# A PSUM evacuation moved ahead of an exponential, the first two blocks moved ahead of the third block's transposes, and narrower attention-value matmuls

## The chip, the cores and the metric

One core of one Trainium2 chip. The time is that of the device, in microseconds (us), from run to run of the same program. A kernel that is compared is run several times in turn with the kernel before on the same chip. Each run also lists the mean clock that TensorE was granted (1 is full speed). A run more than 1.5% above the fastest of its kernel counts as slow and stays out of the ratios.

Engines are named as the profile names them: PE is TensorE's matmuls, PEld its weight loads, ACT is ScalarE, DVE is VectorE, POOL is GpSimd, SP is SyncE. L203 is line 203 of a kernel.

## The reference, cut to what matters

Attention with 4 sink keys and a window of 128 keys, followed by a highway layer on the result:

```python
# q, k, v: (4, 8, 768, 64); n_sink = 4, window = 128; w_h, w_t: (512, 512)
scores = scale * np.matmul(q, k.transpose(0, 1, 3, 2))
keep = is_sink | in_window
scores = np.where(keep, scores, -1e9)
a = np.exp(scores - max); a = a / sum(a)
x = np.matmul(a, v)                      # then (B, S, H*D) as (3072, 512)
H = np.maximum(x @ w_h, 0.0)
T = 1.0 / (1.0 + np.exp(-(x @ w_t + b_t)))
return T * H + (1.0 - T) * x
```

## The kernel before

The 3,072 tokens are 24 blocks of 128, six for each of the four sequences. Block `n` sees itself and block `n-1`; from the third block of a sequence on it also sees the four sink keys. The stages of a block are spread over five iterations of one loop (`pe_T` of block `n` at `i = n-2`, `dve_d` at `i = n+2`), and the program fixes the order of each engine's instructions:

```python
for i in range(-2, NB + 2):
    if has_sink(i): act_sink(i)          # ACT L226: exponential of the sink scores of i, i+1
    if on(i + 1):
        pe_S(i + 1, 0)                   # PE  L243: scores of four heads
        act_S(i + 1, 0)                  # ACT L251: first exponential
        pe_S(i + 1, 1)
    ...pe_X(i - 1); act_X(i - 1)         # PE  L310 transposes x; ACT L315 copies xT
    for o in os_: dve_d(o)               # DVE L342: reads hps (block i-2)
    if on(i): dve_mask(i, 1)
    if on(i + 1): act_S(i + 1, 1)        # ACT L251: second exponential
    if on(i + 2): pe_T(i + 2)            # PE  L196/L198: transposes q, k into tp
    ...
    if on(i): pe_A(i)                    # PE  L277: attention-value; L283: its sink part
    if on(i + 2): act_T(i + 2)           # ACT L203: q/k copy, tp -> SBUF
    ...dve_mask(i + 1, 0); dve_rec(i); dve_o(i - 2); dve_x(i)
    for m in ms:                         # m = i-1
        pe_Mt(m)                         # PE  L321/L323 -> tps
        act_u(m)                         # ACT L329: tanh, reads tps
        pe_Mh(m)                         # PE  L336 -> hps
    if has_sink(i + 1): pe_sink(i + 1)   # PE  L221 -> sk, two blocks at once
```
(cut; the comments are not in the kernel)

Two more things matter. The PSUM pool `m` has two buffers of one bank, which `xtp`, `tp`, `tps`, `hps` and, in two blocks of six, `sk` take in turn. And each of the 16 attention-value matmuls of a block streams `_AVN` columns, of which the result needs 65:

```python
_AVN = 112
m_ps = ctx.enter_context(tc.tile_pool(name="ps_m", bufs=2, space=PSUM))
...
nc.tensor.matmul(av[:, g, 2 * hl + hh, 0:_AVN], lhsT=e[:, hh, hl, pc, :],
                 rhs=vt[:, 65 * h:65 * h + _AVN], ...)
```

The softmax here doesn't subtract the row's maximum and nothing guards it: scores larger than these inputs give would overflow.

Of the kernel before, what the change touches and what calls it, by code (L numbers as in the profile page):

```python
# [13 lines left out]

_EXP_BIAS = math.log(1.9)

_AVN = 112


@with_exitstack  # L20
def kernel(
# [37 lines left out]
    AHEAD = 8  # L59
# [65 lines left out]
    def load_sink_v(b):  # L125
        nc.gpsimd.dma_start(out=vs_dn[b % 2], in_=v[b, :, 0:NSINK, :])
# [38 lines left out]
    def more_constants():  # L165
        nc.vector.memset(bt16, 0.0)
        nc.vector.memset(ones_row, 0.0)
        nc.vector.memset(ones_row[0:1, :], 1.0)
        for i in range(2):
            nc.vector.memset(ks_bd[i], 0.0)  # L170
            nc.vector.memset(vs_bd[i], 0.0)
            nc.vector.memset(es_t[i], 0.0)
        nc.vector.tensor_copy(out=mask0, in_=mask[:, 1, :])
        nc.vector.memset(mask0[0:NSINK, :], 1.0)
        nc.vector.tensor_copy(out=mask1, in_=mask)
        nc.vector.memset(mask1[0:NSINK, 0, :], 1.0)
        nc.vector.tensor_scalar_mul(bt16[0:1, :], bt32, 0.5)
# [6 lines left out]
    def warm_up(n):  # L184
        w = m_ps.tile([P, DM], FP32, tag="m", name="wps")
        for _ in range(n):
            nc.tensor.matmul(w, lhsT=warm[:, 0:P], rhs=warm, start=True, stop=True)

    qkT, tp_of, s_of, e_of, av_of, rec_of = {}, {}, {}, {}, {}, {}
    xtp_of, xh_of, xT_of, t_of, u_of, h_of, dd_of, ee_of, sk_of = {}, {}, {}, {}, {}, {}, {}, {}, {}  # L190

    def pe_T(n):
        qsd, ksd = qk_sd.pop(n)
        tp = m_ps.tile([P, 2 * NHP, P], FP16, tag="m", name="tp")
        for j in range(NHP):
            nc.tensor.transpose(tp[:, j, :], qsd[:, 2 * j:2 * j + 2, :], ident)  # L196
        for j in range(NHP):
            nc.tensor.transpose(tp[:, NHP + j, :], ksd[:, 2 * j:2 * j + 2, :], ident)  # L198
        tp_of[n] = tp

    def act_T(n):
        qk = qkT_pool.tile([P, 2 * NHP, P], FP16, tag="qk", name="qk")
        nc.scalar.copy(out=qk, in_=tp_of.pop(n))  # L203
        qkT[n] = (qk[:, 0:NHP, :], qk[:, NHP:2 * NHP, :])
# [20 lines left out]
    def act_sink(n):  # L225
        nc.scalar.activation(out=es_t[(n // 2) % 2][0:NS4], in_=sk_of.pop(n)[0:NS4], func=AF.Exp,  # L226
                             bias=ebias[0:NS4], scale=SCALE)

    def srcs_of(n):
        return ([] if n % NSC == 0 else [qkT[n - 1][1]]) + [qkT[n][1]]  # L230

    def pe_S(n, g):
        qT, _ = qkT[n]
        srcs = srcs_of(n)
        np_ = len(srcs)
        sps = s_ps.tile([P, 2, 512], FP32, tag="s", name="sps")
        for hl in range(2):
            hp = 2 * g + hl
            for pc, kk in enumerate(srcs):
                for hh in range(2):  # L240
                    rows = slice(64 * hh, 64 * hh + 64)
                    o = (hl * np_ + pc) * P
                    nc.tensor.matmul(sps[:, hh, o:o + P], lhsT=kk[rows, hp, :],  # L243
                                     rhs=qT[rows, hp, :], start=True, stop=True)
        s_of[n, g] = sps

    def act_S(n, g):
        np_ = 1 if n % NSC == 0 else 2
        sps = s_of.pop((n, g))
        e = e_pool.tile([P, 2, 2, np_, P], FP16, tag="e", name="e")  # L250
        nc.scalar.activation(out=e.rearrange("p a b c d -> p a (b c d)"),  # L251
                             in_=sps[:, :, 0:2 * np_ * P], func=AF.Exp,
                             bias=ebias, scale=SCALE)
        e_of[n, g] = e

    def dve_mask(n, g):
        c = n % NSC
        np_ = 1 if c == 0 else 2
        m = {0: mask0, 1: mask1.rearrange("p a b -> p (a b)")}.get(
            c, mask.rearrange("p a b -> p (a b)"))  # L260
        ev = e_of[n, g].rearrange("p a b c d -> p (a b) (c d)")
        nc.vector.tensor_tensor(  # L262
            out=ev, in0=ev, in1=m.unsqueeze(1).to_broadcast([P, 4, np_ * P]),
            op=ALU.mult)
# [24 lines left out]
    def dve_rec(n):  # L289
        rec = r_pool.tile([P, H], FP32, tag="rec", name="rec")  # L290
        nc.vector.reciprocal(out=rec.unsqueeze(2), in_=av_of[n][:, :, 64:65])
        rec_of[n] = rec
# [13 lines left out]
    def pe_X(n):  # L306
        xh = xh_of[n]
        xtp = m_ps.tile([P, NOC, P], FP16, tag="m", name="xtp")
        for j in range(NOC):
            nc.tensor.transpose(xtp[:, j, :], xh[:, j * P:(j + 1) * P], ident)  # L310
        xtp_of[n] = xtp

    def act_X(n):
        xT = x_pool.tile([P, NOC, P], FP16, tag="xT", name="xT")
        nc.scalar.copy(out=xT, in_=xtp_of.pop(n))  # L315
        xT_of[n] = xT
# [15 lines left out]
    def pe_Mh(n):  # L332
        xT = xT_of.pop(n)
        hps = m_ps.tile([P, DM], FP32, tag="m", name="hps")
        for kc in range(NOC):
            nc.tensor.matmul(hps, lhsT=xT[:, kc, :], rhs=wh_sb[:, kc, :],  # L336
                             start=(kc == 0), stop=(kc == NOC - 1))
        h_of[n] = hps

    def dve_d(n):  # L340
        dd = td_pool.tile([P, DM], FP16, tag="dd", name="dd")
        nc.vector.scalar_tensor_tensor(out=dd, in0=h_of.pop(n), scalar=0.0, in1=xh_of[n],  # L342
                                       op0=ALU.max, op1=ALU.subtract)
        dd_of[n] = dd

    def dve_e(n):
        ee = td_pool.tile([P, DM], FP16, tag="ee", name="ee")
        nc.vector.scalar_tensor_tensor(out=ee, in0=u_of.pop(n), scalar=1.0, in1=dd_of.pop(n),  # L348
                                       op0=ALU.add, op1=ALU.mult)
        ee_of[n] = ee  # L350

    def dve_o(n):
        otok = o_pool.tile([P, DM], FP32, tag="otok", name="otok")
        nc.vector.scalar_tensor_tensor(out=otok, in0=xh_of.pop(n), scalar=2.0, in1=ee_of.pop(n),  # L354
                                       op0=ALU.mult, op1=ALU.add)
        nc.sync.dma_start(out=out[n * P:(n + 1) * P, :], in_=otok)

    def on(n):
        return 0 <= n < NB
# [4 lines left out]
    def highway(i):  # L364
        return [m for m in range(NB) if m + lag(m) == i]

    def has_sink(n):
        return on(n) and n % NSC >= 2 and n % 2 == 0

    with tc.manual_schedule(engines={ENG.PE, ENG.DVE, ENG.Activation, ENG.SP, ENG.Pool}):  # L370
        for i in range(-2, NB + 2):
            ms, os_ = highway(i), highway(i - 1)
            if i == -2:
                warm_up(8)
                more_constants()
            if has_sink(i):
                act_sink(i)
            if on(i + 1):
                pe_S(i + 1, 0)
                act_S(i + 1, 0)  # L380
                pe_S(i + 1, 1)
            if on(i - 1) and i - 1 not in XBAR:
                pe_X(i - 1)
                act_X(i - 1)
            for o in os_:
                dve_d(o)
            if on(i):
                dve_mask(i, 1)
            if on(i + 1):
                act_S(i + 1, 1)  # L390
            if on(i + 2):
                pe_T(i + 2)
            for o in os_:
                dve_e(o)
            if on(i):
                pe_A(i)
            if on(i + 2):
                act_T(i + 2)
            if on(i + 1):
                dve_mask(i + 1, 0)  # L400
            if on(i):
                dve_rec(i)
            for o in os_:
                dve_o(o)
            if on(i):
                dve_x(i)
                if i in XBAR:
                    sp_X(i)
            for m in ms:
                pe_Mt(m)  # L410
                act_u(m)
                pe_Mh(m)
            if has_sink(i + 1):
                pe_sink(i + 1)
            if i == 0:
                sink_ones()
                sink_v(0, nc.vector)
            if on(i + 2) and (i + 2) % NSC == 0:
                b = (i + 2) // NSC
                pool_sink(b)  # L420
                if b:
                    sink_v(b, nc.gpsimd)
                if b + 1 < B:
                    load_sink_v(b + 1)
            for n in (range(3, AHEAD + 1) if i == -2 else [i + 2 + AHEAD]):
                if n < NB:
                    if n > 3:
                        load_qk(n)
                    load_v(n)
# [35 lines left out]
```

## Time and profile before

146.31 us, median of three runs (146.3 to 146.74).

| what | before | how read |
|---|---|---|
| busiest engine | PE, 80% of the span | the page, part 1 |
| ACT | 68% | the page, part 1 |
| PE at half clock | about 11 to 26 us (the prediction reads 28) | the page, row PEclk (a digit is 3.6 us); the H matmuls at 26.65 us are at the full rate again |
| six blocks, steady | 30.0 us | from one sink exponential to the same of the next sequence |

The profile's page of the kernel before, parts 1 and 2: busy time by engine, then tenths of PE's time and of its clock in 40 equal slices.

```profile
PE 115.4 (80%) x1312; PEld 74.8 (52%) x1312; DVE 96.9 (67%) x214; ACT 98.0 (68%) x129; POOL 73.6 (51%) x98
...
PE   6632069989889988988899789889897988998840
...
PEclk9975555899999999999999999999999999999996
```

No engine is full, so something makes them wait for each other. The list of waits of the kernel before says who; its columns are the total us, the times, and the longest:

```profile
DVE dd L342 <- PE hps L336: 26.2, 24, 1.5
...
ACT e L251 <- PE sps L243: 12.7, 16, 0.9
...
PE hps L336 <- ACT qk L203: 9.4, 17, 0.7
...
ACT es L226 <- PE sk L221: 8.1, 8, 1.1
```

And the chain of waits of the kernel before shows the ring, that is, a loop of waits that closes on itself from block to block; start us, us, what:

```profile
83.15 1.11 ACT e L251
84.26 0.47 ACT xT L315
84.74 1.02 ACT e L251
85.75 0.91 ACT qk L203
...
86.71 1.02 PE hps L336 x4
87.73 0.46 PE sk L221 x8
...
88.24 0.35 issue
```

ACT does first exponential, xT copy, second exponential, q/k copy. Only then may PE do the H matmuls, because `hps` takes the buffer of `tp`. The next scores stand behind the H matmuls, and the next first exponential waits for these scores. That is 4.96 us per block, 5.4 where a sink matmul and its exponential come in between. At the start, PE stands still; its timeline of the kernel before, where the last bracket is the idle time and what ended it:

```profile
18.77 0.61 PE L196 MATMUL tp<-ident,qsd 128*128 128x128 f16 x4 [6.70 <-DMA qsd<-in_q_dram]
```

PE works in program order, so the attention of blocks 0 and 1, whose data is long there, stands behind the transposes of block 2, whose q lands at 18.7 us.

### The profile page before, as it was taken

How to read it: one execution, taken by the hardware profiler on the slowest of the kernel's cores; microseconds unless marked ns; L12 is line 12 of the kernel's file. 1: busy time of each engine (PE TensorE's matmuls, PEld its weight loads, DVE VectorE, ACT ScalarE, POOL GpSimd, SP SyncE). 2: the span in 40 equal slices, each digit the busy share in tenths (PEclk: the TensorE clock that was granted, in tenths of full speed). 3: DMA queues.
4: the chain of work that ended last, by engine and by line, in shares of the span. 5: the costliest groups of instructions: out<-in, count | busy, mean ns of one | idle time of the engine just before them, and what ended most of it. 6: DMA issues, size and time to landing. Idle time of an engine off the chain costs nothing.

```text
span 145.0 us, 3266 instructions
## 1 busy us (share of the span) xinstructions
PE 115.4 (80%) x1312; PEld 74.8 (52%) x1312; DVE 96.9 (67%) x214; ACT 98.0 (68%) x129; POOL 73.6 (51%) x98
## 2 busy tenths in 40 slices
PE   6632069989889988988899789889897988998840
PEld 2122058557646654765666358458464664664410
DVE  7441016578659856966868687678677866968770
ACT  3176029497787877977976797798769778976310
POOL 6999599999969999735099770000300000000000
PEclk9975555899999999999999999999999999999996
DMA  1999999999999999999929999210221021021111
GB/s 10 113 112 168 165 155 158 153 156 197 163 190 195 191 183 150 195 194 152 74 74 147 150 197 161 73 73 3 75 77 72 1 77 72 0 77 72 72 72 72
DMA packets 79728, 17.00 MB, mean 117 GB/s; under 512 B 75617, under 2 KB 76641, under 8 KB 79714
## 3 DMA queue, kind: packets, MB, share of 16 engines
q0 software_dynamic: 76256, 10.51, 107.8%
q1 hardware_dynamic: 3458, 6.30, 12.1%
q8 instruction: 10, 0.16, 0.4%
q14 instruction: 4, 0.03, 0.1%
HBM read 21.01 MB, written 6.29 MB: 188 GB/s over the span
## 4 chain that ended last, share of the span: by engine, by line
ACT 41%; PE 35%; POOL 7%; DMA 5%; issue 5%; DVE 4%; POOLq 0%; DVEq 0%
ACT e L251 25%; PE hps L336 16%; ACT qk L203 11%; DMA ksd<-in_k_dram 5%; PE tps L323 4%; ACT xT L315 4%; PE av L277 4%; PE sps L243 4%; DVE dd L342 3%; PE sk L221 3%; POOL qsd L85 2%; PE tps L321 1%; POOL ksd L86 1%; POOL v L93 1%; PE tp L198 1%
## 5 line engine op out<-in xcount | busy, mean ns | idle before, releaser
L251 ACT ACTIVATE e<-sps,ebias 128x1024 f16<-128x1024 f32 (+1 forms) x48 | 49.8, 1041 | 12.7 <-PE sps L243 12.7
L342 DVE SCALAR_TENSOR_TENSOR dd<-hps,xh 128x512 f16<-128x512 f32 x24 | 16.6, 692 | 26.2 <-PE hps L336 26.2
L262 DVE TENSOR_TENSOR e<-e,mask 128x1024 f16<-128x1024 f16 (+1 forms) x48 | 30.7, 640 | 4.4 <-ACT e L251 4.0
L203 ACT COPY qk<-tp 128x1024 f16<-128x1024 f16 x24 | 24.3, 1015 | 11.7 <-PE tp L198 11.7
L336 PE MATMUL hps<-wh_sb,xT 128*128 128x512 f16 x96 | 24.6, 378 | 9.4 <-ACT qk L203 9.4
L85 POOL DMA_DIRECT2D qsd<-in_q_dram x24 | 22.4, 932 | 7.6 <-PE tp L198 5.0
L323 PE MATMUL tps<-wt_sb,xT 128*128 128x512 f16 x96 | 25.0, 383 | 0.0
L277 PE MATMUL av<-v,e 128*128 128x112 f16 x352 | 24.4, 218 | 0.7 <-DVE e L262 0.7
L86 POOL DMA_DIRECT2D ksd<-in_k_dram x24 | 22.2, 925 | 1.1 <-PE av L283 1.0
L93 POOL DMA_DIRECT2D v<-in_v_dram x24 | 22.5, 937 | 0.0
L277 PEld LDWEIGHTS <-e 128*128 128x128 f16 x352 | 21.3, 101 | 1.1 <-DVE e L262 0.9
L336 PEld LDWEIGHTS <-xT 128*128 128x128 f16 x96 | 9.3, 97 | 23.5 <-issue 14.1
L329 ACT ACTIVATE u<-tps 128x512 f16<-128x512 f32 x24 | 14.7, 613 | 6.9 <-PE tps L323 6.8
L243 PE MATMUL sps<-qk 64*128 64x128 f16 x352 | 14.8, 225 | 2.6 <-ACT qk L203 2.6
L348 DVE SCALAR_TENSOR_TENSOR ee<-u,dd 128x512 f16<-128x512 f16 x24 | 16.5, 686 | 0.2
L296 DVE TENSOR_TENSOR xh<-av,rec 128x512 f16<-128x512 f32 x24 | 16.4, 685 | 0.1
L196 PE MATMUL tp<-ident,qsd 128*128 128x128 f16 x96 | 9.9, 230 | 7.2 <-DMA qsd<-in_q_dram 6.9
L354 DVE SCALAR_TENSOR_TENSOR otok<-xh,ee 128x512 f32<-128x512 f16 x24 | 15.6, 648 | 0.1
L243 PEld LDWEIGHTS <-qk 64*128 64x128 f16 x352 | 10.7, 98 | 9.4 <-issue 7.3
L323 PEld LDWEIGHTS <-xT 128*128 128x128 f16 x96 | 9.5, 99 | 11.0 <-issue 1.8
L315 ACT COPY xT<-xtp 128x512 f16<-128x512 f16 x24 | 13.7, 572 | 1.0 <-PE xtp L310 1.0
L212 POOL COPY ks<-qk 64x16 f16<-64x16 f16 x8 | 1.6, 201 | 21.1 <-ACT qk L203 20.9
(49 smaller groups left out, 103.3 us busy)
## 6 DMA issues: line engine op xcount, KB each, us to landing
out_dram<-otok SPq DMA_DIRECT2D x24, 256.0 KB, 2.2
qsd<-in_q_dram POOLq DMA_DIRECT2D x24, 128.0 KB, 5.7
ksd<-in_k_dram POOLq DMA_DIRECT2D x24, 128.0 KB, 5.7
v<-in_v_dram POOLq DMA_DIRECT2D x24, 128.0 KB, 6.1
wt_sb<-in_moe_w_t_dram POOLq DMA_DIRECT2D x1, 512.0 KB, 6.7
wh_sb<-in_moe_w_h_dram POOLq DMA_DIRECT2D x1, 512.0 KB, 8.8
vd<-in_v_dram POOLq DMA_DIRECT2D x4, 4.0 KB, 4.2
bt<-in_moe_b_t_dram SPq DMA_DIRECT2D x1, 2.0 KB
```

Source lines behind the costliest of these rows:

```text
L85: nc.gpsimd.dma_start(out=qsd, in_=q[b, :, rows, :].transpose([1, 0, 2]))
L86: nc.gpsimd.dma_start(out=ksd, in_=k[b, :, rows, :].transpose([1, 0, 2]))
L93: nc.gpsimd.dma_start(out=vt[:, :, 0:D], in_=v[b, :, rows, :].transpose([1, 0, 2]))
L203: nc.scalar.copy(out=qk, in_=tp_of.pop(n))
L243: nc.tensor.matmul(sps[:, hh, o:o + P], lhsT=kk[rows, hp, :], rhs=qT[rows, hp, :], start=True, stop=True)
L251: nc.scalar.activation(out=e.rearrange("p a b c d -> p a (b c d)"), in_=sps[:, :, 0:2 * np_ * P], func=AF.Exp, bias=ebias, scale=SCALE)
L262: nc.vector.tensor_tensor(out=ev, in0=ev, in1=m.unsqueeze(1).to_broadcast([P, 4, np_ * P]), op=ALU.mult)
L277: nc.tensor.matmul(av[:, g, 2 * hl + hh, 0:_AVN], lhsT=e[:, hh, hl, pc, :], rhs=vt[:, 65 * h:65 * h + _AVN], start=first, stop=False, skip ...
L315: nc.scalar.copy(out=xT, in_=xtp_of.pop(n))
L323: nc.tensor.matmul(tps, lhsT=xT[:, kc, :], rhs=wt_sb[:, kc, :], start=False, stop=(kc == NOC - 1))
L336: nc.tensor.matmul(hps, lhsT=xT[:, kc, :], rhs=wh_sb[:, kc, :], start=(kc == 0), stop=(kc == NOC - 1))
L342: nc.vector.scalar_tensor_tensor(out=dd, in0=h_of.pop(n), scalar=0.0, in1=xh_of[n], op0=ALU.max, op1=ALU.subtract)
```

## The change

Three parts. (1) The q/k copy goes ahead of the second exponential on ACT, so that `tp`'s buffer comes free sooner. (2) Up to block 2 the loop is rearranged, so that blocks 0 and 1 are done while block 2's loads are under way. (3) `_AVN` goes from 112 to 80, to take PE time away.

```diff
-_AVN = 112
+_AVN = 80
...
-            if on(i + 1):
+            if i >= 2 and on(i + 1):
                 pe_S(i + 1, 0)
                 act_S(i + 1, 0)
                 pe_S(i + 1, 1)
...
-            if on(i + 1):
+            if i >= 2 and on(i + 2):
+                pe_T(i + 2)
+                act_T(i + 2)
+            if i >= 2 and on(i + 1):
                 act_S(i + 1, 1)
-            if on(i + 2):
-                pe_T(i + 2)
...
                 pe_A(i)
-            if on(i + 2):
-                act_T(i + 2)
...
+            if i == 1:
+                dve_d(0)
+                pe_T(2)
+                act_T(2)
+            if -1 <= i < 2:
+                for g in range(2):
+                    pe_S(i + 1, g)
+                    act_S(i + 1, g)
+                dve_mask(i + 1, 0)
+            if i < 2:
+                n = {-2: 0, -1: 1, 1: 3}.get(i)
+                if n is not None:
+                    pe_T(n)
+                    act_T(n)
```
(cut; the rest follows from it: the guards on what is done early, and the loads of blocks 10 and 11, which keep their order)

More of the change, by code (lines that the diff above doesn't have):

```diff
@@ L385 @@
             for o in os_:
-                dve_d(o)
+                if o not in dd_of:
+                    dve_d(o)
             if on(i):
                 dve_mask(i, 1)
-            if on(i + 1):
+            if i >= 2 and on(i + 2):
+                pe_T(i + 2)
+                act_T(i + 2)
+            if i >= 2 and on(i + 1):
                 act_S(i + 1, 1)
-            if on(i + 2):
-                pe_T(i + 2)
             for o in os_:
@@ L396 @@
                 pe_A(i)
-            if on(i + 2):
-                act_T(i + 2)
-            if on(i + 1):
+            if i >= 2 and on(i + 1):
                 dve_mask(i + 1, 0)
@@ L424 @@
                     load_sink_v(b + 1)
-            for n in (range(3, AHEAD + 1) if i == -2 else [i + 2 + AHEAD]):
+            for n in {-2: range(3, AHEAD + 1), 0: [], 1: [10, 11]}.get(i, [i + 2 + AHEAD]):
                 if n < NB:
```

## The prediction

> **What bounds it now.** No engine is full: busy shares on the page are PE 80%, ACT 68%, DVE 67%, POOL 51%. The chain that ended last is ACT 41%, PE 35%. In the steady part it is a ring through both, read from the chain of waits at 83 to 88 us: first exponential 1.11, xT copy 0.47, second exponential 1.02, q/k copy 0.91, then the H matmuls (L336) 1.02, then the next scores 0.35: 4.96 us per block. The matmuls wait for the q/k copy ("PE hps <- ACT qk" 9.4 us, 17 times, in the list of waits): the PSUM pool "m" has two buffers, and hps takes the one that tp leaves. With a sink matmul it is 5.4, so a pair of blocks with a sink takes 10.4 (first exponentials at 78.19, 88.59, 98.95); six blocks take 30.0 (68.92 to 98.95). Loads don't bind after the start: POOL needs 2.7 us a block. At the start PE has nothing from 12.1 to 18.8 us, waiting for block 2's q, and runs at half clock from about 11 to 28 us.
>
> **The change, costed.**
> 1. q/k copy ahead of the second exponential. Mh may start 1.02 us earlier, so the ring above is cut. Next limits, walked by hand with the trace's durations: (a) ACT back to back: 1.00 + 0.47 + 0.91 + 1.02 + 0.52 = 3.9 us; (b) PE/DVE: Mh 1.05, dd 0.74, transposes 0.44, attention-value, tps 1.08: tp now waits for dd, because dd frees its buffer; (c) xT copy to tps to hps to scores: 1.0 + 0.6 + 1.08 + 0.86 + 0.35 = 3.9. A block without sink: 3.9 to 4.1. A price: the sink matmul needs the PSUM buffer that tanh reads, and tanh is now behind the second exponential, so sink and its exponential no longer hide: about 5.05 with sink. Pair with sink 10.4 -> 9.0; six blocks 30.0 -> 26.0. Over the 20 blocks of the steady part (28.5 to 129 us): -13.5 us, nearly all critical.
> 2. 80 columns: 16 matmuls now start 49 ns apart (0.79 us per block). The Trainium skill, "TensorE: Matmul & The Clock Gate", section "Back-to-back issue gap", gives N/2.4 + 2.5 ns warm: 49 for 112 columns, which this trace confirms; 36 for 80 (estimate; scores go at 28, so weight loads needn't stop it). -0.21 us a block of PE, in ring (b) only: alone about nothing before; after step 1 up to 0.2 us in about half of the blocks (counted above).
> 3. Blocks 0, 1 early. Attention and highway of block 0 and attention of block 1 move into the 6.7 us hole. First exponential of block 3 comes at about 26.5 to 27 instead of 28.54. Against it: Mt and Mh of block 0 wait for weights (wh lands about 18) ahead of block 2's transposes (+0.4), and PE is still cold. Net -1.5.
> Tail unchanged (-0.2).
>
> 146.3 - 13.5 - 1.5 = 131.3; something for hand-overs: **131.5 us, range 128.5 to 135.5**. Faster 0.97, same 0.025, slower 0.005.
>
> **What would show it.** Wait "PE hps <- ACT qk" nearly gone; "ACT e <- PE sps" (12.7 us) mostly gone without sink; new waits of tp (L196) on dd and of sk on tanh; pairs about 9.0 apart; L277 at about 36 ns start to start; ACT busy share up to about 75%; first transposes of block 2 at about 19.8; H matmuls of block 0 before them.
>
> **What would make it wrong.** L277 limited by its weight loads (stays 50 ns: +1 to 2 us). dd late, so ring (b) binds everywhere (+3). PE staying cold past 30 us because the start is more broken up, or block 4's loads (issued about 19, landing 6 to 8 later) not there at 26.5 (+1 to 2). Exponentials and copies slowed by denser PSUM traffic.

## The result and the profile after

133.65 us, median of four runs (132.22 to 135.34), against 146.31 before (four runs). The run at 135.34 counts as slow and is not in the ratio. The ratio is 0.910, with a 95% interval of 0.9015 to 0.9185. Ratios here are the mean time of one kernel's fast runs over that of the other's of the same rounds, so not quite the ratio of the medians. The prediction of 131.5 us with a range of 128.5 to 135.5 holds it, 2 us above the centre.

The four runs differ more than those before, and with the clock: 132.22 us at a mean clock of 0.994, then 133.19, 134.11 and 135.34 at 0.945, 0.943 and 0.924. The profile was taken of the first, and that of the kernel before of a run of 146.7 us, so the spans below differ by more (14.5 us) than the medians (12.7). The same parts of the page, for the changed kernel:

```profile
PE 111.0 (85%) x1312; PEld 70.0 (54%) x1312; DVE 96.6 (74%) x214; ACT 98.3 (75%) x129; POOL 73.4 (56%) x98
...
PE   6757596399999899999998989999989899997820
...
PEclk9999999999999999999999999999999999999997
```

Busy times hardly moved except PE's (4.4 us less); the span shrank around them. The list of waits of the changed kernel:

```profile
DVE dd L342 <- PE hps L336: 14.9, 24, 2.9
...
ACT es L226 <- PE sk L221: 5.3, 8, 0.7
ACT e L251 <- PE sps L243: 3.5, 6, 0.7
...
PE sk L221 <- ACT u L329: 2.1, 7, 0.3
```

The H matmuls' wait for the q/k copy is gone from the list, and a new one is there, the sink matmul's for tanh (7 times). The chain of waits of the changed kernel over two blocks, the first without a sink matmul at its end, the second with one:

```profile
80.56 0.25 PE tps L321
80.82 0.86 PE tps L323 x4
81.68 0.86 PE hps L336 x4
82.54 0.35 PE sps L243 x8
...
82.92 1.07 ACT e L251
...
84.39 1.03 ACT qk L203
85.42 1.02 ACT e L251
86.44 0.50 ACT u L329
...
86.98 0.61 PE sk L221 x8
```

In the chain the first block is now held by PE, though nearly in a tie (the xT copy, which the tps matmuls also need, ends at 80.39 us, 0.05 before they start), and the second by ACT: tanh stands behind the second exponential, and the sink matmul waits for the buffer that tanh reads. First exponentials start at 78.84, 82.92 and 87.99 us: 4.08 us for the block without, 5.07 for the block with a sink matmul.

To see where the time went, the span is cut at the sink exponentials, of which there are eight. The first cut is the second sink exponential (block 4), the last one is the eighth, 18 blocks later; the timeline of ACT gives them.

| stretch (us) | before | changed | difference |
|---|---|---|---|
| start to second sink exponential | 38.52 | 34.48 | -4.04 |
| 18 blocks, second to eighth | 90.08 | 79.71 | -10.37 |
| eighth to the end | 16.4 | 16.3 | -0.1 |
| span | 145.0 | 130.5 | -14.5 |

The start of the changed kernel's PE timeline shows the hole filled; block 0's highway matmuls stand ahead of block 2's transposes, at half speed:

```profile
15.73 0.63 PE L321 MATMUL tps<-bt,ones_row 128*128 128x512 f16 x1
16.15 1.91 PE L323 MATMUL tps<-wt_sb,xT 128*128 128x512 f16 x4
17.85 1.91 PE L336 MATMUL hps<-wh_sb,xT 128*128 128x512 f16 x4
19.56 0.50 PE L196 MATMUL tp<-ident,qsd 128*128 128x128 f16 x4
```

### The profile page after: what moved, and what is told of

It is laid out like the page before. It is cut to its first block, busy times and chain, and to the rows that moved or that the text cites. A ratio compares the mean times of both kernels' runs of the same rounds, so it can differ in the third digit from the quotient of the medians.

```text
span 130.5 us, 3265 instructions
## 1 busy us (share of the span) xinstructions
PE 111.0 (85%) x1312; PEld 70.0 (54%) x1312; DVE 96.6 (74%) x214; ACT 98.3 (75%) x129; POOL 73.4 (56%) x98
## 4 chain that ended last, share of the span: by engine, by line
PE 44%; ACT 23%; DMA 9%; POOL 9%; issue 6%; DVE 6%; POOLq 0%; DVEq 0%
ACT e L251 13%; PE tps L323 11%; PE hps L336 11%; ACT qk L203 6%; DMA qsd<-in_q_dram 6%; PE sps L243 5%; PE av L277 4%; POOL qsd L85 3%; DMA ksd<-in_k_dram 3%; PE tps L321 3%; DVE dd L342 3%; POOL ksd L86 3%; PE sk L221 3%; POOL v L93 2%; ACT xT L315 2%
## 5 line engine op out<-in xcount | busy, mean ns | idle before, releaser
L323 PE MATMUL tps<-wt_sb,xT 128*128 128x512 f16 x96 | 25.5, 389 | 0.1
L336 PE MATMUL hps<-wh_sb,xT 128*128 128x512 f16 x96 | 25.5, 390 | 0.0
L277 PE MATMUL av<-v,e 128*128 128x80 f16 x352 | 19.6, 204 | 2.3 <-DVE e L262 2.3
L329 ACT ACTIVATE u<-tps 128x512 f16<-128x512 f32 x24 | 14.5, 605 | 7.9 <-PE tps L323 7.8
L277 PEld LDWEIGHTS <-e 128*128 128x128 f16 x352 | 17.0, 100 | 3.2 <-DVE e L262 3.0
L348 DVE SCALAR_TENSOR_TENSOR ee<-u,dd 128x512 f16<-128x512 f16 x24 | 16.4, 685 | 0.2
L296 DVE TENSOR_TENSOR xh<-av,rec 128x512 f16<-128x512 f32 x24 | 16.4, 684 | 0.1
L321 PE MATMUL tps<-bt,ones_row 128*128 128x512 f16 x24 | 9.3, 389 | 1.7 <-ACT xT L315 1.0
L198 PE MATMUL tp<-ident,ksd 128*128 128x128 f16 x96 | 9.7, 226 | 1.0 <-DMA ksd<-in_k_dram 1.0
```

What stands on the lines that cost most here:

```text
L296: nc.vector.tensor_tensor(out=xh.rearrange("p (h d) -> p h d", d=D), in0=av_of.pop(n)[:, :, 0:D], in1=rec_of.pop(n).unsqueeze(2).to_broadc ...
L323: nc.tensor.matmul(tps, lhsT=xT[:, kc, :], rhs=wt_sb[:, kc, :], start=False, stop=(kc == NOC - 1))
L336: nc.tensor.matmul(hps, lhsT=xT[:, kc, :], rhs=wh_sb[:, kc, :], start=(kc == 0), stop=(kc == NOC - 1))
```

## The experiments

Theory: the steady gain is the freed `tp` buffer; narrower columns pay only once PE is on the ring; the start gains what the hole allows, less what PE loses to half clock. Rivals: the gain is PE time; or the run-to-run spread is the loads. All results below were correct against the reference. The table has all twelve runs; "first" is the stretch to the second sink exponential, "18 blocks" the steady one, both from the profiled run alone.

| run | median us | ratio to before, 95% | first | 18 blocks |
|---|---|---|---|---|
| copy_only | 137.56 | 0.9447 (0.9389 to 0.9504) | 38.16 | 81.37 |
| cols_only | 145.98 | 1.0052 (0.9953 to 1.0151) | 37.59 | 89.40 |
| start_only | 144.88 | 0.9951 (0.9901 to 1.0002) | 36.48 | 90.04 |
| all_112 | 136.18 | 0.9348 (0.9297 to 0.9399) | 36.54 | 81.56 |
| copy_80 | 135.3 | 0.9252 (0.919 to 0.9315) | 37.48 | 79.72 |
| all_65 | 133.65 | 0.9135 (0.9078 to 0.9191) | 37.73 | 79.43 |
| after_again | 133.13 | 0.9077 (0.903 to 0.9124) | 36.25 | 79.72 |
| warm | 132.45 | 0.9027 (0.8987 to 0.9067) | 34.56 | 79.72 |
| start_warm | 143.97 | 0.9858 (0.9819 to 0.9898) | 36.00 | 90.03 |
| sink_av | 132.16 | 0.8947 (0.888 to 0.9015) | 37.22 | 77.39 |
| sink_av_late | 132.64 | 0.9043 (0.8987 to 0.91) | 36.30 | 78.43 |
| sink_warm | 130.51 | 0.8896 (0.8849 to 0.8943) | 34.51 | 78.14 |

The runs are from three chips, so across rows the ratios and the 18 blocks are to be compared, less so the medians.

### One part at a time

copy_only, the first part alone on the kernel before:

```diff
+            if on(i + 2):
+                pe_T(i + 2)
+                act_T(i + 2)
             if on(i + 1):
                 act_S(i + 1, 1)
-            if on(i + 2):
-                pe_T(i + 2)
...
-            if on(i + 2):
-                act_T(i + 2)
```

> The kernel before with only the q/k copy put ahead of the second exponential, in every block. Theory (the buffer of tp released 1.0 us sooner lets the H matmuls go): about 138.5 us, the wait of the H matmuls for the q/k copy (9.4 us) nearly gone, and a new wait of the sink matmul for tanh. It stays above the full change by the start (about 2) and by the 112 columns (about 2.8). Rival (the gain needs the shorter attention-value matmuls, that is, PE was the limit): over 142 us.

Measured 137.56. The 18 blocks fell from 90.08 to 81.37, 84% of the steady gain (8.71 of 10.37). The wait of the H matmuls for the q/k copy is not in its list of waits any more, and the sink matmul's for tanh is. PE had the same work as before, so the rival falls.

cols_only, `_AVN = 80` alone:

> The kernel before with 80 columns alone. Theory: the attention-value matmuls are not on the ring of before, so 0 to 0.6 us less (start and tail only), though they start 36 ns apart instead of 49. Rival (PE time bounds): 24 x 0.21 = 5 us less.

Measured 145.98, ratio 1.0052 with an interval on both sides of 1. In the profile the 18 blocks are 0.68 us shorter. Nothing like 5 us is there: 24 blocks times 0.21 us of PE work went into PE's waits.

start_only, the rearranged start alone:

> The full change without the new place of the q/k copy from block 2 on and with 112 columns: only blocks 0 and 1 early. Theory: 1.5 to 2.8 us less than before (143.5 to 144.8), all of it ahead of block 3's first exponential. Rival (the weights of the highway layer hold up block 2's transposes and eat the gain): within 0.7 us of before.

Measured 144.88, 0.7 us under before (means 144.85 and 145.59), short of the 1.5 to 2.8 expected; its interval reaches 1.0002, so a gain is not clear of the noise. The steady blocks are as before (90.04). Its clock row shows what happened after the early blocks:

```profile
PEclk9975589699999999999999999999999999999998
```

The clock came back near 19 us and fell again near 26 (slice 8 of 40 reads 6). Between the first and second sink exponential lie 11.32 us (25.16 to 36.48), where 10.36 is usual in this kernel.

all_112, everything but the columns, and all_65, everything with 65 columns:

> The full change with 112 columns kept. Theory: about 136.5 us: blocks without a following sink matmul are bound by PE, 0.21 us each, 4 in 6; blocks with one are bound by ScalarE and the tanh buffer and pay nothing. Rival (columns do nothing): as the full change, 133.7.

> The full change with 65 columns, the least that the result needs. Theory (these matmuls are bound by their columns): they start 30 ns apart, 0.1 us less a block in the blocks bound by PE, about 1 us less than the full change. Rival (80 is already at the floor of the weight loads): start to start stays at 36 ns and the time as the full change.

all_112 measured 136.18: the columns are worth 1.85 us in the 18 blocks (81.56 - 79.71) once the copy has moved (1.65 from copy_only to copy_80), and 0.68 without. The 2.5 us that the expectation's 0.21 us in four blocks of six comes to was not reached. So the parts don't just add up. copy_80 says the same without the early start:

> The kernel before with the q/k copy moved and 80 columns, without the early blocks 0 and 1. Theory: the columns pay about 2 to 2.5 us once the copy has moved (they paid nothing resolved alone): about 135.2 us; what then remains to the full change, about 2, is the start. Rival (the start gives only the 0.7 that it gave alone): 134.

It measured 135.3, and its 18 blocks take 79.72 us, as in the full change; what is left to the full change is the start alone.

With 65 columns the matmuls do start 30 ns apart, as one sees in PE's timeline of all_65 (eight of them and one L283 in 0.36 us, of which L283 is 0.11):

```profile
86.83 0.41 PE L277 MATMUL av<-v,e 128*128 128x65 f16 x8
87.08 0.28 PE L283 MATMUL av<-vs,es 128*128 128x260 f16 x1
87.19 0.41 PE L277 MATMUL av<-v,e 128*128 128x65 f16 x8
```

But the time is 133.65, no less than the full change (three of its four runs have a mean clock of 0.937 or less, so the stages say more), and the 18 blocks gained 0.3 us. The spacing was expected rightly and the gain wrongly: 80 columns already take these matmuls mostly off the ring. The traces show what holds the blocks after that: with 65 columns the tps matmuls start 0.04 to 0.05 us after the end of the xT copy in five blocks of six (83.50 after 83.46), with 80 already 0.04 to 0.07 after it (80.44 after 80.39), while with 112, in copy_only, they start later, behind the attention-value matmuls (85.23 after 85.01).

### The clock at the start

after_again is the changed kernel itself, once more on another chip; warm adds matmuls of zeros, into PSUM that is overwritten afterwards, where PE waits before block 3:

```diff
+    def fill(dst, n):
+        for _ in range(n):
+            nc.tensor.matmul(dst, lhsT=warm[:, 0:P], rhs=warm[:, 0:dst.shape[-1]],
+                             start=True, stop=True)
...
+        if g == 0 and n in (0, 1, 2):
+            fill(sps[:, 0, :], 5)          # in pe_S
...
+        if n == 1:
+            fill(av[:, 0, :, :].rearrange("p h e -> p (h e)"), 4)   # in pe_A
...
+            if n == 2 and t == 1:
+                fill(sk[:, 1, :], 24)      # in pe_sink
```

> The changed kernel once more, unedited, as the yardstick of this chip. Expected: 132 to 135 us, and the shorter runs are those with the higher mean granted clock (0.99 against 0.94), because in the others PE drops back to half clock for some microseconds around block 3.

> The changed kernel with 43 matmuls of zeros put into the waits of PE ahead of block 3 (results overwritten), to keep PE's clock up. Theory (the spread of the changed kernel is the half clock at the start): clock 0.98 or more in all runs, 132 to 132.8 us, spread under 1 us, about 1 us under the unedited kernel. Rival (the spread comes from elsewhere, such as the loads): median and spread as the unedited kernel, or longer by the added work.

after_again: the three runs at 0.994 or 0.995 took 132.51 to 132.91 us, the three at 0.923 to 0.946 took 133.34 to 135.59 (the last counts as slow). Its profile fell on one of the latter, of 133.97. Clock rows of after_again and of warm:

```profile
PEclk9985569859999999999999999999999999999998
```

```profile
PEclk9999999999999999999999999999999999999996
```

In after_again the first to the second sink exponential takes 10.68 us (25.57 to 36.25), in the run that kept its clock 9.16: the second fall costs 1.5 us there. With warm all six runs had 0.985 or more, the median was 132.45 (131.63 to 132.8), and that stretch took 9.16. So the theory stands for the profiled runs; over all runs it is less clear. The spread of 3.1 us became 1.2, a little over the 1 us expected, but without the slow run it was only 1.5, and the mean of the fast runs fell by 0.7 us (133.09 to 132.36) with overlapping intervals.

Two limits. The mean clock does not sort the runs of other kernels: in cols_only the two at 0.994 and 0.995 took 147.0 and 146.68 us, the two at 0.932 and 0.934 only 145.28 and 144.98, so it is a hint and not a proof for runs without a profile. And something else moves the start too: the first sink exponential, about where the second fall sets in, comes between 25.16 and 26.31 us in the profiles with the new start (without sink_av_late, whose sink is moved); whether that is the loads was not tried.

The first fall cost nothing that showed: the changed kernel ran at half rate until 19.6 us, warm did not, and their first sink exponentials come at 25.32 and 25.40. The Trainium skill, "TensorE: Matmul & The Clock Gate", section "Part 1: The HAM clock gate", says that the clock starts at half and goes to full after some 3.4 us of sustained work, in a window that runs freely, so that it differs from run to run. These runs agree: in after_again and warm the first eight matmuls, of 512 columns, take 3.59 us (from 1.26), the half rate, and by 6.5 us the full one is there (four transposes in 0.40 us); the same program kept its clock in some executions and lost it in others, and 512-column matmuls start 0.43 us apart in the half state (four in 1.70 us, from 16.15 to 17.85 above) and 0.21 in the full one. But those 0.43 us fell in a run whose clock row reads 9 everywhere, so the row misses some; the spacing of the matmuls is the surer sign.

start_warm asks whether this also explains start_only:

> start_only with the 43 matmuls of zeros in the waits at the start. start_only gained only 0.7 us, less than the 1.5 to 2.8 expected; its profile shows half clock at 26 to 29 us and 11.3 us between the first two sink exponentials where 10.4 is usual. Theory (that dip ate the rest): clock 0.98 or more, 10.4 us between them, about 143.9 us or 1 us under start_only (ratio to before about 0.983 to 0.988). Rival (the early blocks are worth no more): as start_only, ratio 0.995.

Measured 143.97, ratio 0.9858, clock 0.988 or more in all six runs, and 10.35 us (25.65 to 36.00) between the first two sink exponentials. All as the theory expected, and its interval (0.9819 to 0.9898) lies under that of start_only (0.9901 to 1.0002), though on another chip. The early blocks alone are worth 0.5% by the ratio, not clear of the noise, and 1.4% with the clock kept.

### The price of the copy's new place

With 80 columns, the attention-value tile has free columns. sink_av writes the sink scores there, so that they take no buffer of pool `m`:

```diff
-        sk = m_ps.tile([P, 2, P], FP32, tag="m", name="sk")
+        sk = av_last[0]                   # the av tile of the block just done
...
-                nc.tensor.matmul(sk[:, t, :], lhsT=ks[:, hp * P:(hp + 1) * P],
-                                 rhs=qT[:, hp, :], ...)
+                nc.tensor.matmul(sk[:, t, :, 80:112], lhsT=ks[:, hp * P:(hp + 1) * P],
+                                 rhs=qT[:, hp, :].rearrange("p (a b) -> p a b", b=32), ...)
```
(cut; the exponential reads the same columns, and the comment is not in the kernel)

The first matmul of the sink scores clears accumulate flags in a bank that holds finished results; the Trainium skill, "PSUM — Partial Sum Buffer", section "The four PSUM rules", says that the flags of the bank are cleared, not the data, and the correct result agrees.

> The changed kernel with the sink scores written to the columns 80 to 112 of the attention-value PSUM tile, which the shorter matmuls leave free, so that they take no buffer of pool m and need not wait for tanh. Theory (the price of the copy's new place is that wait): pairs of blocks with a sink 8.8 us instead of 9.16, 2.4 to 2.8 us less in all; no wait of the sink matmul for tanh. Rival (ScalarE's own order holds the sink exponential back anyway): 0.5 us less or nothing.

> As sink_av, and the sink matmul and its exponential put behind the next block's first scores and exponential. Theory: the first exponential no longer waits for the sink, but the attention-value matmuls now wait for the sink exponential (they reuse its PSUM tile): pairs 8.75 us, about 3 us less than the changed kernel, no more than 0.6 better than sink_av. Rival (that wait is hidden): pairs of 8.4 us, 6 us less.

The changed kernel's ACT timeline around a sink exponential:

```profile
85.30 1.14 ACT L251 ACTIVATE e<-sps,ebias 128x1024 f16<-128x1024 f32 x1
86.31 0.62 ACT L329 ACTIVATE u<-tps 128x512 f16<-128x512 f32 x1
87.62 0.47 ACT L226 ACTIVATE es<-sk,ebias 32x256 f16<-32x256 f32 x1 [0.70 <-PE sk L221]
```

and sink_av's (its lines are shifted: L254, L333, L228):

```profile
86.97 1.14 ACT L254 ACTIVATE e<-sps,ebias 128x1024 f16<-128x1024 f32 x1
87.98 0.62 ACT L333 ACTIVATE u<-tps 128x512 f16<-128x512 f32 x1
88.81 0.47 ACT L228 ACTIVATE es<-av,ebias 32x256 f16<-32x256 f32 x1 [0.22 <-PE av L222]
```

The sink exponential starts 0.83 us after tanh instead of 1.31. Pairs of blocks with a sink take 8.79 us (80.02 to 88.81) instead of 9.16, as expected, and the 18 blocks 77.39 instead of 79.72; no wait of the sink matmul for tanh is in its list of waits any more. That confirms the buffer that tanh reads as a price, of about 0.4 us per sink matmul (2.33 us for six); the rest of the 1 us between a block with and one without is not explained by it. The same section of the clock page as cited above ("Architectural detail") calls ACT's queue strict first-in first-out, and the trace agrees: in both kernels tanh starts only 1.01 us after the exponential ahead of it, though in the changed kernel the last tps matmul was followed by the H matmuls at 85.66, 0.65 us before tanh. The whole time gained less than the 2.4 to 2.8 expected (means of the fast runs 131.69 against 133.09 of after_again). Between the two profiled runs the start took 0.97 us of it back (first stretch 37.22 against 36.25, with the clock falling again in both); whether that holds for the other runs is not shown.

sink_av_late puts the sink behind the next first exponential:

```diff
-            if has_sink(i):
-                act_sink(i)
...
                 pe_S(i + 1, 1)
+            if has_sink(i):
+                pe_sink(i)
+                act_sink(i)
...
-            if has_sink(i + 1):
-                pe_sink(i + 1)
```

It is no better: pairs of 8.97 us (8.75 expected), 18 blocks 78.43. The new wait that was expected is in its list, the attention-value matmuls for the sink exponential, but it is short; the matmuls' weight loads waited longer without a cause that the profile names:

```profile
PEld L280 <- issue: 2.1, 7, 0.7
...
PE av L280 <- ACT es L228: 0.6, 1, 0.6
```

Why it is 0.2 us a pair over what was expected is left open.

sink_warm joins sink_av and the matmuls of zeros:

> Both repairs in one: sink scores in the spare columns of the attention-value tile (with the zeros between the two halves of the first one) and the 43 matmuls of zeros at the start. Theory: the two are in different stages and add up: 132.45 (zeros alone) less 8 pairs x 0.36 = about 129.6 us, clock 0.98 or more. Rival (something else takes over in the steady part): 131 or more.

Measured 130.51 us (129.71 to 131.07), ratio 0.8896: the lowest median here (its interval overlaps that of sink_av), and its interval lies wholly under that of the changed kernel. It is 0.9 above what was expected. In the profiled run 0.74 us of that was one event, seen in DVE's and PE's timeline:

```profile
48.15 1.53 DVE L366 SCALAR_TENSOR_TENSOR ee<-u,dd 128x512 f16<-128x512 f16 x1
...
51.61 0.61 PE L227 MATMUL av<-qk,ks 128*128 128x128 f16 x8 [0.59 <-DVE xh L314]
```

One DVE operation took 1.53 us instead of 0.69, and here the sink matmul has to wait for DVE to be done reading the attention-value tile. A second such operation, at 66.44 us, cost its stretch nothing (17.00 us). Both run while POOL does its tensor operation of L129 (47.69 to 49.13 and 66.04 to 67.41 us). That this is the cause was not tried, and whether it happens in each run is open.

## Why the prediction was right, and where its sum was off

- "hps takes the one that tp leaves" and "the ring above is cut": right. copy_only alone gave 84% of the steady gain.
- "About 5.05 with sink": measured 5.07. The price by tanh's buffer was right in kind, and sink_av took about 0.4 us of it away.
- "A block without sink: 3.9 to 4.1": mis-sized, measured 4.08 to 4.25 for blocks with full-size exponentials, and hence six blocks took 26.57 us (25.32 to 51.89), not 26.0, and the steady part of 20 blocks gave 11.6 us (100.44 - 88.87), not 13.5. The term that failed is in ring (c), "0.86 + 0.35" for the H matmuls and the scores up to the next exponential. From the start of the H matmuls to that exponential the changed kernel takes 1.40 us (81.52 to 82.92), not 1.21. The kernel before has the same 1.40 (81.75 to 83.15), so the prediction could have read it there; its chain shows 1.02 + 0.35, which was shortened by hand. Of the 0.19 missing, 0.10 lies ahead of the first scores: they start 0.96 us after the H matmuls (81.52 to 82.48), and four of these take 4 x 0.216 = 0.86. The other 0.09 lies between the first scores and the exponential, 0.44 us (82.48 to 82.92) and not 0.35. The one block of six at 4.25 goes through ring (b), as the prediction allowed for some blocks: in the chain, `dd` at 91.74 us (0.70) releases the transposes at 92.49.
- "80 columns", 49 ns to 36: right. Eight of them and one L283 take 0.40 us (83.77 to 84.17), of which L283 is 0.11. "Alone about nothing": right.
- "Net -1.5" at the start: too small where the clock holds (28.16 to 25.32 for the first sink exponential, 2.84 us in this pair of profiles; over the four with the old start and the nine with the new one, again without sink_av_late, the means are 28.14 and 25.65) and about right where it falls again, which the prediction listed as what would make it wrong; warm and start_warm show it.
- "Tail unchanged (-0.2)": -0.1.

Together: 1.9 us too much in the steady part, 1.3 too little at the start, and about 1.5 for the second clock fall, which by their mean clocks three runs of four had (only one of each kernel's runs has a profile). That makes up the 2 us between 131.5 and 133.65; the 1.5 is measured in after_again and carried over. That the centre came so near is in part luck, since the first two errors offset each other.

The mis-sized term, in PE's timeline of the changed kernel:

```profile
81.52 1.03 PE L336 MATMUL hps<-wh_sb,xT 128*128 128x512 f16 x4
...
82.48 0.62 PE L243 MATMUL sps<-qk 64*128 64x128 f16 x16
...
84.80 1.03 PE L323 MATMUL tps<-wt_sb,xT 128*128 128x512 f16 x4
85.66 1.03 PE L336 MATMUL hps<-wh_sb,xT 128*128 128x512 f16 x4
```

The Trainium skill, "TensorEngine Tiling (Array Packing)", section "Key Properties", says that PE drains when the tiling mode changes. The scores use 64 rows, the H matmuls 128, and the trace agrees: no such gap lies between groups that both use 128 rows (the H matmuls at 85.66 start 0.86 after the tps matmuls at 84.80). That the drain is the cause was not tried.

## What to carry to other kernels

Where a rotating pool of PSUM has few buffers, ask of each evacuation which later matmul takes its buffer, and put the copy that a matmul waits for ahead of work that nobody waits for; then ask the same of what was pushed back, since here the price (tanh, and behind it the sink matmul) was predictable and partly avoidable. A cut in an engine's work pays only once that engine is on the ring: the same 80 columns saved 0.7 us in 18 blocks before the move and 1.7 after it (81.37 to 79.72). When work is moved into a hole at the start, look at the clock afterwards: matmuls of zeros in the remaining waits cost nothing that showed here, and the spread was 1.2 us with them and 3.1 without (1.5 without its slow run).

## What the Trainium skill lacked or had wrong

- "TensorE: Matmul & The Clock Gate", section "Back-to-back issue gap": it gives about 81 ns for N=128 and 131 ns for N=512 as what pairs of weight load and matmul sustain in a real kernel, and calls N/2.4 + 2.5 the isolated gap. Here, with a weight load ahead of every matmul, the gaps are 55 ns at 128 (0.22 us for four), 0.216 us at 512 (0.86 for four), 49 at 112, 36 at 80 and 30 at 65: the formula holds, the two figures do not.
- The same page, section "Why this matters for your kernels": it asks for no PE-idle gaps over about 3 us. In after_again the clock fell near 25.5 us although PE's longest wait in the 8 us before was 1.8 us, and in warm, where the waits were filled, it did not. Which waits set the fall off was not tried.
- "TensorEngine Tiling (Array Packing)", "Key Properties": no figure for the drain at a change of tiling mode. Here 0.10 us lies between the H matmuls and the scores, and as much between sink scores and scores (86.98 to 87.52 us is 0.54 for eight that otherwise take 8 x 0.055 = 0.44), if the drain is its cause.
- No page says that the recorded clock can read full while matmuls run at half speed; here it did, with 512-column matmuls 0.43 us apart in a run of mean clock 0.994. The clock page does warn that these records are unreliable.
